# Attention and expert routing on one core: keys of the first batch in four parts, its value products on two column halves, a constant's cast later, row subtractions on VectorE

## Chip, cores, metric

One core of one Trainium2 chip. The metric is the time of one execution on the device in microseconds, the median of the runs of a kernel.

## What is computed

```python
B, N, C = (4, 10048, 128); n_agents = 49
def sm(a, b):                                   # softmax of scaled scores
    s = scale * (a @ b.transpose(0, 2, 1))
...
a2k = sm(agents, k)
agent_v = a2k @ v
q2a = sm(q, agents)
x = q2a @ agent_v                               # 4 x 10048 rows of 128
...
# 4 groups of 4 experts: the best group, in it the best expert, by x @ w_group and x @ w_expert
h = np.maximum(xg[mask_e] @ w1[g, e], 0.0)      # 128 -> 1024
ye = h @ w2[g, e]                               # 1024 -> 128
out[tok_idx] = combined[:, None] * ye
```

The inputs q, k and agents are drawn with a spread of 0.8.

## The kernel before

Each batch is 79 tiles of 128 rows, handled in ten chunks of eight tiles. Products are made of float16 halves: `xh` is the float16 cast of a float32 tile (ScalarE), `xl` the rest (a subtraction, on VectorE or GpSimd, called POOL in the profile), and three matmuls stand for one exact product. Only the sums of exp(scores) times values (`at<-vf,S`) and a few small steps are float32 matmuls; the profile records two instructions for each of these.

A batch has an agent part (scores of the keys, maximum, exponentials `S`, value products), then the choice of the expert that most rows take, that expert's first matrix multiplied by the agents' values (`at<-w1f,at`, giving `wbuf`), and a query part per chunk: scores, `mq` and `ef` (VectorE), exponential (ScalarE), `rows` as high and low half, transposes of `rows` (`at<-ident,rows`), `et`. Then come natural tiles of 512 rows, in eight units each: `first` (line 914) makes two matmuls `ph<-et,wbuf`, `hh` on ScalarE and `hl` on VectorE; `second` (line 930) twelve matmuls `po`. A unit is second up to LAG = 8 units after it was first. The agent and query parts of batch b+1 are woven into the units of batch b. TensorE's, and in the front VectorE's and ScalarE's, instructions keep the order in which the program is written; every engine takes its queue in order.

Only the first batch has nothing to be woven into. Its agent part, the **front** (line 396), is written out in the table ORDER, which sets the order on TensorE, VectorE, ScalarE and of the loads. A letter is a step, the digit a chunk or a part:

- k, v, q: loads of keys, values and the first query chunk. h: the cast to `xh`. l: the subtraction `xl`, on POOL for chunks 1 and 4. s: scores of a key chunk. S: their copy to memory for chunks 3 to 6. M: the chunk's maximum `mch`.
- x, T, a, b, B: a part's maximum: over its chunks (`mx`), transposed by TensorE (`at<-cp,mx`), over its rows (`ma`), spread to all rows by TensorE (`at<-cp,ma`), copied (`mbs`).
- u, e, p, P: subtract the part's maximum, exponential, value products of the first four and of the other tiles. A part has its own sum in PSUM (`acc`), and c adds the parts up with their weights w into `a0`.
- Z, y, r, g, G, t: the first query chunk; g sums its weights over rows on TensorE, between the value products.
- z: that many matmuls of the identity with itself that nobody reads. They write to columns 384 to 511 of the PSUM tile `last`, which also holds the last part's sum.
- A: `main_soon` (line 800): from `a0` the average row, its expert, and that expert's loads `w1f` and `w2f`, issued by SyncE after it has read the choice `which`. D, W, F, R: the agents' values scaled, the expert's matrix, logits and routing of the first chunk. n: steps of the later query chunks.

Parts are of three, three and four chunks. A part's sum is 49 rows high, so a product uses 49 of TensorE's 128 columns; in the agent parts of the other batches (line 365) even tiles go to columns 0 to 48 and odd ones to columns 64 to 112, and the two sums are added at the end.

`query_split` (line 623) makes the high half of `rows` on ScalarE, and for all chunks but the front's first its low half on POOL in pieces of three tiles. POOL also makes all the `xl` of queries. Lines 1238 to 1240, behind the front, load a constant `uf` into a buffer of the tag that `ef` uses (two buffers) and cast it to `upper`, which only the last batch reads (line 987).

In the profile all operations of TensorE, VectorE and ScalarE carry the line of a helper, 138.

## Time and profile before

| | before |
|---|---|
| median of 3 runs | 982.96 us (982.53 to 990.22) |
| profiled execution | 982.84 us, of which the span of the trace is 981.0 us |
| TensorE busy | 923.2 us, 94% of the span |
| VectorE busy | 710.6 us, 72% |
| ScalarE busy | 592.1 us, 60% |
| POOL busy | 420.5 us, 43% |
| granted TensorE clock | 0.99 of full over the span |

A row of the waits says which engine and tile stood, behind "<-" what released it. In the timeline a row is one instruction or a run of equal ones: its start, its duration, and in brackets the idle time of the engine before it and what ended that. Rows of a timeline overlap a little, since an instruction starts before the one ahead of it has drained.

### The profile page before, as it was taken

The numbers are of one execution on the slowest core, as the hardware profiler recorded it, in microseconds if no ns is written. First come the engines' busy times: TensorE is split into PE (matmuls) and PEld (weight loads), VectorE is DVE, ScalarE is ACT, GpSimd is POOL, SyncE is SP. The second block draws the span as 40 slices with busy tenths as digits, with TensorE's granted clock in tenths as the row PEclk, the third lists the DMA queues.
The fourth block names the chain that finished last, engine by engine and source line by source line (L and its number), as shares of the span: only waits on it lengthen the run. The fifth ranks groups of instructions, "written<-read, shape, count | busy, mean of one in ns | idle before, by whom it ended". The sixth has DMA issues, their size and how long they took to land.

```text
span 981.0 us, 30672 instructions
## 1 busy us (share of the span) xinstructions
PE 923.2 (94%) x12943; PEld 721.8 (74%) x12943; DVE 710.6 (72%) x1389; ACT 592.1 (60%) x1073; POOL 420.5 (43%) x681
## 2 busy tenths in 40 slices
PE   7979999999999999999999999999999988989996
PEld 6847887788778788887887788777766656657675
DVE  6677889866987866689785666999976546545563
ACT  5365686777567667856764687564445445434452
POOL 3252465363036244303620452000073786886854
PEclk9988999999999999999999999999999999999998
DMA  9573344630185552018653311134135333433321
GB/s 326 199 250 118 87 149 148 208 122 24 39 297 191 154 161 77 24 37 298 219 153 107 89 41 32 54 143 152 33 120 200 114 117 91 127 99 110 104 79 39
DMA packets 63443, 125.88 MB, mean 128 GB/s; under 512 B 6727, under 2 KB 40904, under 8 KB 60352
## 3 DMA queue, kind: packets, MB, share of 16 engines
q1 hardware_dynamic: 58944, 117.92, 36.0%
q0 software_dynamic: 4352, 5.91, 2.5%
q8 instruction: 103, 1.69, 0.7%
q14 instruction: 44, 0.36, 0.1%
HBM read 90.35 MB, written 33.75 MB: 126 GB/s over the span
## 4 chain that ended last, share of the span: by engine, by line
PE 67%; DVE 12%; issue 3%; ACT 2%; DMA 1%; POOL 1%; another core or an unknown queue 1%; SPq 0%; DVEq 0%; ACTq 0%
PE po L138 34%; PE ph L138 22%; PE at L138 11%; DVE hl L138 5%; DVE oo L138 1%; DMA xf<-kT 1%; DMA w2f<-w 1%; DVE oa L138 1%; POOL xl L257 0%; DVE oh L138 0%; ACT hh L138 0%; DVE mch L138 0%; DVE rd L138 0%; DVE pt L138 0%
## 5 line engine op out<-in xcount | busy, mean ns | idle before, releaser
L138 DVE SCALAR_TENSOR_TENSOR hl<-ph,hh 128x512 f16<-128x512 f32 (+1 forms) x656 | 436.8, 680 | 199.0 <-ACT hh L138 155.6
L138 PEld LDWEIGHTS <-hh 128*128 128x128 f16 x5200 | 423.9, 97 | 167.2 <-issue 22.6
L138 ACT ACTIVATE hh<-ph 128x512 f16<-128x512 f32 (+1 forms) x656 | 378.9, 593 | 247.9 <-PE ph L138 223.0
L138 PE MATMUL po<-wbuf,hh 128*128 128x128 f16 x4816 | 477.1, 219 | 12.5 <-issue 11.6
L138 PE MATMUL po<-wbuf,hl 128*128 128x128 f16 x2408 | 437.4, 219 | 4.1 <-issue 4.0
L138 PE MATMUL ph<-et,wbuf 98*128 98x512 f16 (+1 forms) x1040 | 308.8, 380 | 5.6 <-DVE hl L138 3.3
L257 POOL TENSOR_TENSOR xl<-xf,xh 128x256 f16<-128x256 f32 x280 | 181.3, 679 | 301.0 <-ACT xh L138 294.4
L138 PEld LDWEIGHTS <-hl 128*128 128x128 f16 x2600 | 253.2, 97 | 12.6 <-issue 11.4
L1129 POOL DMA_INDIRECT er<-erow,gidx x68 | 69.6, 1024 | 123.1 <-DVE over L138 110.0
L138 PEld LDWEIGHTS <-wbuf 98*128 98x128 f16 x1216 | 93.2, 99 | 22.8 <-issue 18.8
L138 ACT ACTIVATE xh<-xf 128x1024 f16<-128x1024 f32 x78 | 81.5, 1045 | 42.5 <-PE at L138 32.3
L1166 POOL DMA_INDIRECT out<-oo,sidx x68 | 67.7, 996 | 55.4 <-DVE oo L138 45.2
L633 POOL TENSOR_TENSOR rows<-ef,rows 128x147 f16<-128x147 f32 (+2 forms) x117 | 47.0, 430 | 52.2 <-ACT rows L138 47.1
L138 PEld LDWEIGHTS <-xh 128*128 128x128 f16 x1264 | 55.8, 96 | 5.4 <-issue 3.6
L138 PE MATMUL ph<-ets,wbuf 98*128 98x512 f16 x176 | 53.3, 379 | 0.9 <-issue 0.8
L138 PE MATMUL at<-vf,S 128*49 128x129 f32 (+1 forms) x632 | 52.5, 277 | 1.1 <-ACT S L138 1.1
L1145 POOL MEMSET gap<- 128x320 f16 x136 | 52.3, 385 | 0.3
L138 PEld LDWEIGHTS <-xl 128*128 128x128 f16 x632 | 50.0, 96 | 2.5 <-DVE xl L138 1.3
L138 PE MATMUL at<-agh,xh 128*128 128x49 f16 x545 | 50.8, 184 | 0.8 <-DVE wbuf L138 0.8
L138 DVE TENSOR_TENSOR oo<-po,cw 128x512 f32<-128x512 f32 x65 | 43.9, 675 | 10.4 <-remote 7.2
L138 PE MATMUL at<-agh,xl 128*128 128x49 f16 x545 | 50.6, 184 | 0.3 <-POOL xl L257 0.3
L138 PE MATMUL at<-agl,xh 128*128 128x49 f16 x545 | 50.5, 184 | 0.0
(272 smaller groups left out, 818.5 us busy)
## 6 DMA issues: line engine op xcount, KB each, us to landing
xf<-qT SPq DMA_DIRECT2D x38, 512.0 KB
vf<-v SPq DMA_DIRECT2D x36, 516.0 KB
xf<-kT SPq DMA_DIRECT2D x35, 512.0 KB
out<-oo SPq DMA_DIRECT2D x62, 256.0 KB
wbuf<-wall SPq DMA_DIRECT2D x11, 1024.0 KB
wsg<-wall SPq DMA_DIRECT2D x6, 1024.0 KB
erow<-rows SPq DMA_DIRECT2D x3, 1975.0 KB
w2f<-w SPq DMA_DIRECT2D x7, 512.0 KB
```

Of the source, the lines that this page charges most:

```text
L138: y = f(*a, **k)
L257: eng.tensor_sub(out=xl[:, y], in0=xf[:, y], in1=xh[:, y])
L633: (vec if early else pool).tensor_sub(out=rows[:, w, NA:2 * NA], in0=ef[:, y], in1=rows[:, w, 0:NA])
L1129: ins = pool.indirect_dma_start(out=er[:, q], out_offset=None, in_=erow[b][:, :], in_offset=bass.IndirectOffsetOnAxis(ap=place(b, j * w + ...
L1145: tc.keep_in_program_order(pool.memset(gap, 0.0))
L1166: ins = pool.indirect_dma_start(out=out, out_offset=bass.IndirectOffsetOnAxis(ap=place(x["b"], x["j"] * n + q)[1], axis=0), in_=o[:, q], i ...
```

## The change

- The keys' parts are of one, two, three and four chunks, so that the first part's maximum is known after one chunk; ORDER is written anew for it (its last part is that of before). T makes a second copy of the transposed maxima on partitions 64 to 112, so that maxima, weights and sums stand on both column halves.
- Value products of the front go in turn to columns 0 to 48 and 64 to 112; `a0` is then 113 rows high, and `main_soon` adds its halves by one more float32 matmul with `two` (an identity above an identity) before it goes on. Three halves of PSUM tiles are zeroed at the start.
- A step i is new: 30 matmuls of the identity, written to another PSUM tile, ahead of `at<-w1f,at` (W).
- The load of `uf` and the cast to `upper` go to the end of batch 1's routing.
- The low halves of `rows` of query chunks 1 to 3 of the first batch are made by VectorE in one instruction each.

```diff
+SIDES = HALF + NA
-PARTS = [3, 3, 4]
+PARTS = [1, 2, 3, 4]
+FIRST = 3
-ORDER = ("z44 k0 h0 k1 l0 h1 k2 s0 z8 l1 h2 k3 M0 l2 h3 k4 s2 z6 l3 h4 v0 s1 M2 s3 z10 l4 M1 k5 S3 x0 M3 T0 z8 a0 h5 "
+ORDER = ("z44 k0 h0 k1 l0 h1 k2 s0 z8 l1 h2 k3 v0 M0 T0 z6 a0 l2 b0 z6 B0 h3 k4 s2 z6 u0 e0 l3 h4 s1 p0 M2 s3 l4 P0 M1 k5 S3 x1 "
...
-         "t0 D2 n10 D1 n5 W2 D2 F0 n2 R0").split()
+         "t0 D2 n10 D1 n5 i30 W2 D2 F0 n2 R0").split()
 def front(b, early, order, later):
-        ma, wt, mm, a0, se = [early.tile([NA, w], F32, name=name) for name, w in (("ma", n), ("wt", n), ("mm", 1), ("a0", C + 1), ("se", 1))]
+        ma, wt, mm, a0 = [early.tile([SIDES, w], F32, name=name) for name, w in (("ma", n), ("wt", n), ("mm", 1), ("a0", C + 1))]
-        acc = [(both, both, last)[i][0:NA, y:y + C + 1] for i, y in enumerate((0, C + 1, 0))]
+        acc = [(both, both, both, last)[i][0:SIDES, y:y + C + 1] for i, y in enumerate((0, C + 1, 2 * C + 2, 0))]
+        for x in both, last, small:
+            vec.memset(x[HALF // 2:HALF], 0.0)
...
             elif o == "T":
-                pe.transpose(small[0:NA, 0:P], hold["x"], identf)
+                x = hold["x"] if PARTS[c] > 1 else mch[:, ends[c] - 1]
+                pe.transpose(small[0:NA, 0:P], x, identf)
+                pe.matmul(small[HALF:SIDES, 0:P], x, identf, start=True, stop=True)
...
-                    pe.matmul(acc[i], S[0:m, t], vfs[c % 6][0:m, t - t0], start=todo[i] == whole[i], stop=todo[i] == 1)
+                    side = t % 2 * HALF
+                    pe.matmul(acc[i][side:side + NA], S[0:m, t], vfs[c % 6][0:m, t - t0], start=todo[i] > whole[i] - 2, stop=todo[i] < 3)
...
+            elif o == "i":
+                busy(c, psT[:, 384:512])
 def query_split(b, ci, x, early):
-        for i in range(0, t1 - t0, t1 - t0 if early else 3):
+        whole = early or b == 0 and ci <= FIRST
+        for i in range(0, t1 - t0, t1 - t0 if whole else 3):
...
-            (vec if early else pool).tensor_sub(out=rows[:, w, NA:2 * NA], in0=ef[:, y], in1=rows[:, w, 0:NA])
+            (vec if whole else pool).tensor_sub(out=rows[:, w, NA:2 * NA], in0=ef[:, y], in1=rows[:, w, 0:NA])
 def main_soon(b, early, a0, se, busy):
-        vec.tensor_scalar(out=za, in0=a0[:, C:C + 1], scalar1=1e-9, scalar2=None, op0=ALU.add)
+        ps, psT = bank(b), bank(1)
+        whole = psT[0:NA, P:P + C + 1]
+        pe.matmul(whole, two[0:SIDES], a0, start=True, stop=True)
+        busy(BUSY[0])
+        vec.tensor_scalar(out=za, in0=whole[:, C:C + 1], scalar1=1e-9, scalar2=None, op0=ALU.add)
         vec.reciprocal(out=za, in_=za)
-        vec.tensor_mul(out=se, in0=se, in1=za)
-        ps, psT = bank(b), bank(1)
-        pe.matmul(ps[:, 0:1], a0[:, 0:C], se, start=True, stop=True)
+        av = sm.tile([NA, C], F32, name="av")
+        vec.tensor_scalar(out=av, in0=whole[:, 0:C], scalar1=za, scalar2=None, op0=ALU.mult)
+        pe.matmul(ps[:, 0:1], av, se, start=True, stop=True)
         busy(BUSY[0])
-        av = sm.tile([NA, C], F32, name="av")
-        vec.tensor_scalar(out=av, in0=a0[:, 0:C], scalar1=za, scalar2=None, op0=ALU.mult)
 def rest(b):
         yield from routing(b, 0, NTP)
+        if b == 1:
+            uf = wk.tile([P, P], F32, name="uf", tag="ef")
+            sync.dma_start(out=uf, in_=cpk[:, CUSED:CUSED + P])
         yield from main_of(b, NTP)
+        if b == 1:
+            vec.tensor_copy(out=upper, in_=uf)
...
-    uf = wk.tile([P, P], F32, name="uf", tag="ef")
-    sync.dma_start(out=uf, in_=cpk[:, CUSED:CUSED + P])
-    vec.tensor_copy(out=upper, in_=uf)
```

VectorE near the start of the front, from the first chunk's subtraction `xl` to the subtractions of the part's maximum (`S<-ph,mbs`), before:

```order
L138 TENSOR_TENSOR xl<-xf,xh 128x1024
L138 TENSOR_REDUCE mch<-ph 128x49
L138 TENSOR_TENSOR xl<-xf,xh 128x1024 x2
L138 TENSOR_REDUCE mch<-ph 128x49 x2
L138 TENSOR_REDUCE mx<-mch 128x49
L138 TENSOR_REDUCE mch<-po 128x49
L138 TENSOR_REDUCE ma<-at 49x1
L138 COPY mbs<-at 128x49
L138 TENSOR_TENSOR S<-ph,mbs 128x392
```

The same place after the change:

```order
L140 TENSOR_TENSOR xl<-xf,xh 128x1024
L140 TENSOR_REDUCE mch<-ph 128x49
L140 TENSOR_REDUCE ma<-at 113x1
L140 TENSOR_TENSOR xl<-xf,xh 128x1024
L140 COPY mbs<-at 128x49
L140 TENSOR_TENSOR S<-ph,mbs 128x392
L140 TENSOR_TENSOR xl<-xf,xh 128x1024
L140 TENSOR_REDUCE mch<-ph 128x49 x2
L140 TENSOR_REDUCE mx<-mch 128x49
L140 TENSOR_REDUCE mch<-po 128x49
L140 TENSOR_REDUCE ma<-at 113x1
L140 COPY mbs<-at 128x49
```

One more `ma`, one more `mbs` and the first chunk's `S` stand between the subtractions `xl`; `ma` waits there for TensorE's two transposes.

VectorE at the end of the front, from the query chunks' maxima `mq` to the first unit's `hl`, before:

```order
L138 TENSOR_REDUCE mq<-at 128x8 x2
L138 TENSOR_TENSOR ef<-at,mq 128x392
L138 TENSOR_TENSOR wbuf_104<-at,wbuf_104 128x512 x2
L138 TENSOR_TENSOR rh<-at,rh 98x20
L138 TENSOR_SCALAR main_959<-cp,at 128x16
L138 SCALAR_TENSOR_TENSOR hl<-ph,hh 128x512
```

And after the change:

```order
L140 TENSOR_REDUCE mq<-at 128x8 x2
L140 TENSOR_TENSOR ef<-at,mq 128x392 x2
L140 TENSOR_TENSOR rows<-ef,rows 128x8x49 x2
L140 TENSOR_TENSOR wbuf_104<-at,wbuf_104 128x512 x2
L140 TENSOR_TENSOR rh<-at,rh 98x20
L140 TENSOR_SCALAR main_1001<-cp,at 128x16
L140 SCALAR_TENSOR_TENSOR hl<-ph,hh 128x512
```

Chunk 2's `ef` and the low halves of `rows` of chunks 1 and 2 now stand ahead of the expert's matrix.

POOL from the cast of the first query chunk's `rows` on, before (four `xl` are a chunk, three `rows` are a chunk):

```order
L627 CAST rows<-ef 128x8x49
L257 TENSOR_TENSOR xl<-xf,xh 128x256 x12
L633 TENSOR_TENSOR rows<-ef,rows 128x3x49 x2
L633 TENSOR_TENSOR rows<-ef,rows 128x2x49
L633 TENSOR_TENSOR rows<-ef,rows 128x3x49 x2
L633 TENSOR_TENSOR rows<-ef,rows 128x2x49
L257 TENSOR_TENSOR xl<-xf,xh 128x256 x12
```

And after the change:

```order
L637 CAST rows<-ef 128x8x49
L259 TENSOR_TENSOR xl<-xf,xh 128x256 x24
L644 TENSOR_TENSOR rows<-ef,rows 128x3x49 x2
L644 TENSOR_TENSOR rows<-ef,rows 128x2x49
L259 TENSOR_TENSOR xl<-xf,xh 128x256 x4
```

The six chunks' `xl` follow each other, and the first `rows` that POOL makes are those of chunk 4.

## Rows read from the trace of the kernel before

**Rows 1.** Busy time of each engine (instructions) by stretch, granted clock, DMA share, GB/s.

```profile
20.00:30.00 10.00, 10.00 (x152) 8.70 (x151) 9.09 (x17) 6.29 (x10) 0.00 (x0) 1.00 1.02 402
30.00:44.00 14.00, 13.77 (x150) 12.45 (x147) 6.72 (x18) 4.71 (x10) 5.61 (x9) 1.00 0.51 180
44.00:54.91 10.91, 7.62 (x85) 5.12 (x85) 5.23 (x24) 4.48 (x8) 3.69 (x7) 0.84 0.51 163
54.91:60.05 5.14, 4.96 (x77) 3.24 (x76) 4.29 (x21) 4.08 (x9) 0.00 (x0) 1.00 0.97 361
60.05:72.04 11.99, 9.03 (x112) 6.34 (x112) 9.74 (x26) 9.76 (x19) 7.34 (x12) 0.86 0.61 205
72.04:82.00 9.96, 6.97 (x48) 4.84 (x48) 4.76 (x12) 4.50 (x10) 4.85 (x10) 0.66 0.47 152
82.00:100.00 18.00, 18.00 (x261) 14.40 (x259) 15.71 (x40) 11.61 (x23) 3.83 (x7) 1.00 0.27 83
```

**Rows 2.** Waits of TensorE, 46 to 82 us: us in total, times, longest.

```profile
PE at L138 <- POOL rows L633: 3.0, 1, 3.0
PE at L138 <- DVE rd L138: 2.9, 1, 2.9
```

**Rows 3.** Timeline of VectorE in the front.

```profile
15.63 0.27 DVE L138 TENSOR_REDUCE ma<-at 49x1 f32<-49x128 f32 x1
16.42 0.21 DVE L138 COPY mbs<-at 128x49 f32<-128x49 f32 x1 [0.51 <-PE at L138]
...
25.62 0.57 DVE L138 TENSOR_REDUCE mch<-ph 128x49 f32<-128x392 f32 x1 [0.50 <-PE ph L138]
...
32.56 0.21 DVE L138 COPY mbs<-at 128x49 f32<-128x49 f32 x1 [0.86 <-PE at L138]
...
43.81 0.34 DVE L138 SCALAR_TENSOR_TENSOR a<-at,wt,a 49x129 f32<-49x129 f32 x1 [4.12 <-PE at L138]
...
45.25 0.16 DVE L138 COPY xs<-po 128x1 f32<-128x1 f32 x1 [0.34 <-PE po L138]
...
61.33 1.23 DVE L138 SCALAR_TENSOR_TENSOR wbuf<-w2f,wbuf 128x1024 f16<-128x1024 f32 x1
```

**Rows 4.** Value products, groups by form: the front, 0 to 45 us.

```profile
L138 PE MATMUL at<-vf,S 128*49 128x129 f32 x156 | 19.5, 275 | 0.8 <-ACT S L138 0.8
```

**Rows 5.** The same group in the next batch, on two column halves, 165 to 225 us.

```profile
L138 PE MATMUL at<-vf,S 128*49 128x129 f32 x156 | 10.5, 277 | 0.3 <-ACT S L138 0.3
```

**Rows 6.** Timeline of ScalarE: exponential of the first query chunk.

```profile
36.38 0.53 ACT L138 ACTIVATE ef<-ef 128x392 f32<-128x392 f32 x1 [0.84 <-DVE ef L138]
```

**Rows 7.** Timeline of TensorE: step z, the step after `a0`, transposes of chunk 2's rows.

```profile
42.93 0.84 PE L138 MATMUL at<-ident 128*128 128x128 f16 x12
44.86 0.35 PE L138 MATMUL po<-se,a 49*128 49x1 f32 x2 [1.09 <-DVE se L138]
...
62.96 0.68 PE L138 MATMUL at<-ident,rows 128*98 128x128 f16 x4 [2.91 <-DVE rd L138]
```

**Rows 8.** The sums of step g: group by form, 0 to 45 us.

```profile
L138 PE MATMUL at<-ones,ef 128*49 128x1 f32 x16 | 0.9, 183 | 0.0
```

**Rows 9.** The expert's matrix by form: 46 to 56 us, then 265 to 285 us.

```profile
L138 PE MATMUL at<-w1f,at 128*128 128x512 f32 x4 | 3.6, 1062 | 1.8 <-DMA w1f<-w 1.8
...
L138 PE MATMUL at<-w1f,at 128*128 128x512 f32 x4 | 2.2, 632 | 0.3 <-DVE hl L138 0.3
```

**Rows 10.** Timeline of POOL: rows of chunk 2, then `xl`, then rows of chunk 3.

```profile
61.43 2.21 POOL L633 TENSOR_TENSOR rows<-ef,rows 128x147 f16<-128x147 f32 x3 [8.30 <-ACT rows L138]
...
69.42 5.15 POOL L257 TENSOR_TENSOR xl<-xf,xh 128x256 f16<-128x256 f32 x8 [3.27 <-issue]
74.53 1.18 POOL L633 TENSOR_TENSOR rows<-ef,rows 128x147 f16<-128x147 f32 x3
```

**Rows 11.** Busy time as in group 1, from the first logits to the fourteenth unit's `hl`.

```profile
54.91:80.90 25.99, 19.86 (x223) 13.60 (x223) 18.48 (x56) 17.86 (x34) 11.25 (x19) 0.81 0.65 223
```

**Rows 12.** Timeline of ScalarE: rows of chunk 3, high half.

```profile
71.59 0.53 ACT L138 ACTIVATE rows<-ef 128x392 f16<-128x392 f32 x1
```

More of the change, by code (lines that the diff above doesn't have):

```diff
@@ L383, in agents_of @@
         ps = bank(b)
-        both = slice(0, HALF + NA)
-        pe.matmul(ps[:, 0:NA], av[both, C:C + 1].broadcast_to([HALF + NA, P]), two[both], start=True, stop=True)
+        both = slice(0, SIDES)
+        pe.matmul(ps[:, 0:NA], av[both, C:C + 1].broadcast_to([SIDES, P]), two[both], start=True, stop=True)
         pe.matmul(ps[:, NA:2 * NA], av[both, 0:C], two[both], start=True, stop=True)
@@ L401, in front @@
         n = len(PARTS)
-        ma, wt, mm, a0, se = [early.tile([NA, w], F32, name=name) for name, w in (("ma", n), ("wt", n), ("mm", 1), ("a0", C + 1), ("se", 1))]
+        ma, wt, mm, a0 = [early.tile([SIDES, w], F32, name=name) for name, w in (("ma", n), ("wt", n), ("mm", 1), ("a0", C + 1))]
+        se = early.tile([NA, 1], F32, name="se")
         mbs = early.tile([P, n, NA], F32, name="mbs")
@@ L419, in columns, with busy @@
             return ps[:, 0:n * NA].rearrange("p (t a) -> p t a", a=NA)
-        def busy(n):
+        def busy(n, to=None):
             for _ in range(n):
-                pe.matmul(last[:, 384:512], ident, ident, start=True, stop=True)
+                pe.matmul(last[:, 384:512] if to is None else to, ident, ident, start=True, stop=True)
         pin = tc.keep_in_program_order
@@ L469, in front @@
             elif o == "T":
-                pe.transpose(small[0:NA, 0:P], hold["x"], identf)
+                x = hold["x"] if PARTS[c] > 1 else mch[:, ends[c] - 1]
+                pe.transpose(small[0:NA, 0:P], x, identf)
+                pe.matmul(small[HALF:SIDES, 0:P], x, identf, start=True, stop=True)
             elif o == "a":
-                vec.tensor_reduce(out=ma[:, c:c + 1], in_=small[0:NA, 0:P], axis=AX.X, op=ALU.max)
+                vec.tensor_reduce(out=ma[:, c:c + 1], in_=small[0:SIDES, 0:P], axis=AX.X, op=ALU.max)
             elif o == "b":
-                pe.matmul(small[:, P:P + NA], ma[:, c:c + 1].broadcast_to([NA, P]), identf[0:NA, 0:NA], start=True, stop=True)
+                pe.matmul(small[:, P:P + NA], ma[0:NA, c:c + 1].broadcast_to([NA, P]), identf[0:NA, 0:NA], start=True, stop=True)
             elif o == "B":
@@ L520, in front @@
             elif o == "D":
-                scaled = scaled or agents_scaled(b, psT)
+                scaled = scaled or agents_scaled(b, psT[:, 0:NA])
                 for _ in range(c):
@@ L629, in query_split @@
             act.activation(rows[:, t0:t1, 0:NA], ef, AF.Copy)
-        for i in range(0, t1 - t0, t1 - t0 if early else 3):
-            y = slice(i, t1 - t0 if early else min(i + 3, t1 - t0))
+        whole = early or b == 0 and ci <= FIRST
+        for i in range(0, t1 - t0, t1 - t0 if whole else 3):
+            y = slice(i, t1 - t0 if whole else min(i + 3, t1 - t0))
             w = slice(t0 + y.start, t0 + y.stop)
-            (vec if early else pool).tensor_sub(out=rows[:, w, NA:2 * NA], in0=ef[:, y], in1=rows[:, w, 0:NA])
+            (vec if whole else pool).tensor_sub(out=rows[:, w, NA:2 * NA], in0=ef[:, y], in1=rows[:, w, 0:NA])
         yield
@@ L829, in main_soon @@
         load_weights(b)
-        return psT[:, 0:NA]
+        return psT
     def main_row(b):
```

6 rows, old and new, of the table ORDER are left out of this document.

## The prediction

> **What bounds the kernel now.** I read the busy time by stretch first. From 82 us on TensorE is busy 18.00 of 18.00 us at the full clock [rows 1], and what follows is the same work before and after the change, so whatever is won ahead of 82 us should reach the end whole. Ahead of it there are three different stretches. Up to 43 us TensorE is full (10.00 of 10 us) with VectorE close behind (9.09) [rows 1]. From 44 to 55 us a chain of short steps runs, in which no engine is half busy except TensorE. From 55 to 82 us no engine is full: TensorE is busy 4.96 + 9.03 + 6.97 = 21.0 of 27.1 us, at a mean clock of 1.00, 0.86 and 0.66 [rows 1]. Busy time times clock gives 5.0 + 7.8 + 4.6 = 17.3 us of work at full clock, so this stretch loses 9.8 us: 6.1 by standing, 3.6 by the half clock, 1.2 GHz, that TensorE has there part of the time.
>
> The waits tell where it stands: 2.9 and 3.0 us [rows 2]. The first is put down to VectorE's `rd`, but what starts at 62.96 are the transposes of chunk 2's `rows` [rows 7], whose low half POOL makes from 61.43 on [rows 10]. POOL had stood idle 8.3 us until ScalarE's high half came. For chunk 3 the high half ended at 71.59 + 0.53 = 72.12 [rows 12], but POOL was in two chunks' `xl` until 74.57 and began the low half at 74.53 [rows 10]: POOL's queue was the cause. After both waits the clock is down: 0.86 and 0.66 [rows 1].
>
> **The change part by part.**
>
> *Value products.* On one column half 156 records, 78 products, take 19.5 us, 0.250 each [rows 4]; on two halves, as the next batch does it, 10.5 us, 0.135 each [rows 5]. So 79 products get 9.1 us cheaper on TensorE, but VectorE takes over as the bound. It waits for TensorE 0.50 and 0.86 us behind long runs of products [rows 3]; these 1.4 us go. It gets one more `ma` and `mbs`, 0.27 + 0.21 = 0.5 us, and near the start it waits for the new part's transposes, at most the 0.5 us that it waits in such a round [rows 3]. Net -0.4 us: between -1.4 (the new steps hidden) and +0.8 (loads or ScalarE's new place for the exponential, ahead of a key chunk's cast, cost besides). So the first query chunk's exponential, which ends at 36.38 + 0.53 = 36.91 [rows 6], ends at 36.5. Its sums on TensorE (0.9) [rows 8], then the 15 products that ORDER puts behind them (15 x 0.135 = 2.0) and step z (0.84) [rows 7] follow: 40.2 us. There the last c starts, which waits for step z because both are in `last`; before it started at 43.81 [rows 3]. **-3.6 us** (-4.6 to -2.4).
>
> One rule speaks against this. The Trainium skill (TensorEngine Tiling, Key Properties) says that changing the tiling mode drains TensorE, and the front changes between full-array scores and halves at every burst of four to eight products. The trace of the next batch, where bursts also stand between full-array matmuls, has no such price left in its 0.135 us [rows 5]; so I go by the row, and keep the case that it fails as a rival.
>
> *main_soon.* The halves are added by a matmul between the last c and `za`. The nearest row is the round from `ma` (ends 15.90) over a small float32 matmul to `mbs` (16.42): 0.52 us [rows 3]. With 129 columns in place of 49, and `av` in place of a one-column product ahead of the next matmul, I take **+0.6 us** (0.4 to 0.9) on the 1.44 us from 43.81 to `xs` at 45.25 [rows 3].
>
> *Step i.* Before `w1f` lands TensorE stands 1.8 us, and the two float32 halves behind that take 3.6 us; with no such wait ahead they take 2.2 [rows 9]. Thirty identity matmuls at 0.84 / 12 = 0.07 [rows 7] are 2.1 us, 0.3 more than the wait. They hide in it but for that 0.3: 3.6 - 2.2 - 0.3, **-1.1 us** (+0.3 if the clock falls all the same, -1.4 if the load lands later). VectorE's and ScalarE's work for chunk 2, which now stands ahead of the expert's matrix, fits into the same wait.
>
> *Rows on VectorE, the constant later.* Chunks 1 and 2 have both halves of `rows` before the expert's matrix, and POOL's queue has no `rows` until chunk 4, so both waits of [rows 2] lose their cause. What is late next? From 54.91 us to the end of the fourteenth unit's `hl`, 26.0 us, VectorE works 18.5, ScalarE 17.9 us [rows 11], and TensorE, by the sum above, about 16 at full clock. VectorE loses chunk 2's `ef` and the cast from this stretch and gets chunk 3's `rows`: even. So it becomes VectorE's stretch: not below 18.5 us. One wait I expect to stay: the first `po` need the low half of the second matrix (1.23 us at 61.33 [rows 3]), which stands behind routing steps on VectorE, so that TensorE stands there for 1 to 2 us; most of that overlaps with VectorE being the bound. I take 19.2 us: **-6.8 us** (-7.5 to -2.4, the latter from the first rival). VectorE's remaining routing work finds room behind 82 us, where it has 18.0 - 15.7 = 2.3 us to spare [rows 1].
>
> *At nothing:* the three zeroings and wider weights (VectorE waits for the first load and for TensorE there), and the cast to `upper` in batch 1: its reader is a whole batch later, and if VectorE should wait for that load, some 2 us, up to eight units already made keep TensorE fed.
>
> Sum: -3.6 + 0.6 - 1.1 - 6.8 = -10.9. The profiled execution took 982.84 us with a span of 981.0, 0.12 below the median of 982.96: 982.84 - 10.9 + 0.12 = 972.1 us. One per cent of the median, about what a measurement of this kernel can tell from no change, is 9.8 us: the line is at 973.1.
>
> **The rivals.**
>
> *The clock falls again.* The wait for the second matrix's low half, and one more behind VectorE at chunk 3's transposes, are as long as the 1.8 us that was followed by half clock before (3.6 against 2.2 us [rows 9]). For it: VectorE's queue is full there. Against it: waits of 0.5 to 1.1 us in the front left the clock at 1.00 [rows 1, 3, 7]. Then two waits of 1.8 us replace 2.9 + 3.0, and the half clock's 3.6 us stay: 2.3 us won in place of 6.8. Sum -6.4: 976.6 us.
>
> *The front hardly moves.* VectorE and the key loads set it (DMA share 1.02 in the stretch [rows 1]), the first query chunk is not earlier but later by 0.8, and the loads of values come late for the last bursts: -1.2 in place of -3.6. Sum -8.5: 974.6 us.
>
> *Halves without gain.* By the rule on draining, the short bursts cost as much as before, 0.250 each. TensorE then stays the front's bound until 43.0, with one round of transposes more, some 1 us: +1.0 in place of -3.6. Sum -6.3: 976.7 us. Against it stands [rows 5].
>
> *Slower than before.* With VectorE the bound, TensorE runs dry again and again between 50 and 82 us and has half clock throughout. Its 17.3 us of work become 34.6 in place of 27.1, +7.5. Sum -3.6 + 0.6 - 1.1 + 7.5 = +3.4: 986.4 us. This decides once waits of some 1.8 us come back every few microseconds; half clock for more than 11 of the 17.3 us of work already eats all the gain. Against it: before, with two waits of 3 us, the mean clock was still 0.86 and 0.66 [rows 1].
>
> **How the numbers follow.** The forecast 0.57, its own range 968.5 to 974.5; the clock 0.20; the front 0.12; halves without gain 0.05; slower 0.03; and 0.03 for more than the sum, its best ends together (-4.6 + 0.4 - 1.4 - 7.5 = -13.1, 969.9 us, and below that only if VectorE's work there shrinks too). The range 967.8 to 978.0 leaves out the slower case and little else. Faster by over 1% (below 973.1): 0.8 of the forecast, a quarter of the front's case, and the 0.03 beyond, 0.46 + 0.03 + 0.03, with a little from the rest: 0.54. Slower by over 1%: 0.03. Within: 0.43.
>
> **What would show it.** Right: value products of the front at 0.135 each; the last c at about 40 us; `w1f`'s halves at 2.2 us with no wait of TensorE ahead; no wait of TensorE for `rows` of chunks 2 and 3; VectorE busy over 0.9 of the stretch between the first logits and the fourteenth `hl`, which lasts 18.5 to 20 us. Wrong: a granted clock well below 1.00 behind 50 us, a wait for `wbuf` or `hl` of 1.8 us and more, or new waits behind 82 us that take the gain back.

## The result and the profile after

| | before | changed |
|---|---|---|
| median | 982.79 us of 4 runs (982.53 to 990.22) | 975.35 us of 4 runs (975.20 to 976.45) |
| span of the profiled execution | 981.0 us | 973.4 us |
| ratio to before, 95% interval | | 0.9894 (0.9855 to 0.9933) |

The forecast was 972.1 us, a ratio of 0.989, within 967.8 to 978.0. The kernel is faster by about one per cent; the span shows 7.6 of the 10.9 us that the steps add up to. The question is where the other 3.3 us went.

First the front. Products of the changed kernel by form, 8 to 42 us, then VectorE's timeline and TensorE's:

```profile
L140 PE MATMUL at<-vf,S 128*49 128x129 f32 x156 | 11.3, 279 | 1.7 <-ACT S L140 1.7
```

```profile
39.59 0.35 DVE L140 SCALAR_TENSOR_TENSOR a<-at,wt,a 113x129 f32<-113x129 f32 x1 [2.45 <-PE at L140]
...
41.70 0.16 DVE L140 COPY xs<-po 128x1 f32<-128x1 f32 x1 [0.53 <-PE po L140]
```

```profile
47.98 2.01 PE L140 MATMUL at<-w1f,at 128*128 128x512 f32 x4
...
50.76 0.17 PE L140 MATMUL at<-rh,et 98*128 98x21 f16 x1 [0.63 <-ACT rh L140]
```

A product takes 11.3 / 78 = 0.145 us in place of 0.250 [rows 4]. The last c starts at 39.59 (before 43.81 [rows 3]), the expert's matrix takes 2.0 us in place of 3.6 [rows 9], and the first logits come at 50.76 in place of 54.91 us: 4.15 earlier. Terms one to three of the prediction's sum said 4.1.

Behind them the two kernels have to be compared over the same work. The marks are each tile's `oo`, VectorE's last step for 512 finished rows: the first is at 84.61 us before and 71.53 after, the tenth at 186.44 and 176.70. From the first logits to the tenth both kernels run 1853 matmuls. Busy time and clock from the first logits to the first `oo`, from there to the tenth, and over both, columns as in [rows 1]; before, then changed:

```profile
54.91:84.61 29.70, 23.57 (x285) 16.55 (x285) 21.24 (x66) 20.24 (x38) 12.84 (x22) 0.83 0.57 196
84.61:186.44 101.83, 98.51 (x1572) 79.82 (x1570) 91.23 (x206) 72.95 (x140) 45.66 (x78) 1.00 0.44 133
54.91:186.44 131.53, 122.08 (x1853) 96.37 (x1853) 112.47 (x271) 93.19 (x177) 58.51 (x99) 0.96 0.47 148
```

```profile
50.76:71.53 20.77, 18.80 (x282) 14.17 (x282) 19.87 (x59) 17.92 (x35) 8.85 (x15) 1.00 0.82 285
71.53:176.70 105.17, 99.01 (x1578) 79.90 (x1575) 94.35 (x214) 73.52 (x140) 46.32 (x78) 1.00 0.43 131
50.76:176.70 125.94, 117.82 (x1853) 94.07 (x1853) 114.22 (x272) 91.44 (x175) 55.17 (x93) 1.00 0.50 157
```

Length less TensorE's busy time is how long it stood. To the first `oo`: 6.1 us before, 2.0 after, and the clock rises from 0.83 to 1.00; with nearly the same matmuls, 285 and 282, the stretch is 8.9 us shorter. Behind it the opposite, at the full clock in both: 105.17 in place of 101.83 us, 2.8 us more standing (6.2 in place of 3.3) and 0.5 us more busy time. VectorE has 3.1 us more work there (94.35 in place of 91.23). Over both, 131.53 becomes 125.94: 5.6 us, of which only 1.3 are standing. The other 4.3 are busy time, the same matmuls at a clock of 1.00 in place of 0.96. The waits of TensorE in the whole stretch, before (the two of [rows 2] stand above these) and after:

```profile
PE ph L138 <- DVE mch L138: 1.4, 2, 1.1
PE ph L138 <- DVE hl L138: 1.2, 1, 1.2
PE at L138 <- ACT rh L138: 0.6, 1, 0.6
PE at L138 <- ACT S L138: 0.3, 1, 0.3
PE at L138 <- POOL xl L257: 0.3, 1, 0.3
```

```profile
PE ph L140 <- DVE hl L140: 2.1, 3, 1.2
PE at L140 <- POOL xl L259: 1.4, 4, 0.5
PE po L140 <- DVE wbuf L140: 1.1, 1, 1.1
PE at L140 <- DVE ma L140: 0.9, 1, 0.9
PE ph L140 <- DVE mch L140: 0.9, 2, 0.5
PE at L140 <- ACT S L140: 0.8, 1, 0.8
PE at L140 <- ACT rh L140: 0.6, 1, 0.6
PE at L140 <- DVE hl L140: 0.4, 1, 0.4
PE at L140 <- DVE rows L140: 0.4, 1, 0.4
```

The waits of 2.9 and 3.0 us are gone; in their place come 0.8 us for `rows` and `hl` (the rows with `at`), 1.1 for the second matrix, 2.0 more for `hl` (with `ph`) and `xl`, and 1.4 more for `ma` and `S`. So the first `oo` is 13.1 us ahead of before, the tenth 9.7. Two more places take from that. From 440 to 465 us, where the third batch starts, it goes from 9.85 to 9.06. And between 735 and 750 us, at the switch to the last batch's kept tiles, it goes from 9.0 at the `oo` of 700 us to 7.2 at that of 747 us, two marks up to which the matmuls of the two kernels differ by the same number. The switch (the first matmul on a kept tile, `ph<-ets,wbuf`) is at 744.3 us before and at 735.0 after. The stretch around it, before, then after, same columns:

```profile
740.00:745.00 5.00, 3.63 (x46) 2.67 (x45) 2.63 (x4) 1.29 (x3) 4.06 (x6) 1.00 0.95 388
745.00:750.00 5.00, 4.20 (x41) 2.50 (x40) 1.43 (x3) 2.06 (x5) 1.54 (x2) 1.00 0.78 241
```

```profile
735.00:740.00 5.00, 4.80 (x23) 2.55 (x23) 0.37 (x2) 0.78 (x2) 2.56 (x3) 0.56 0.70 215
740.00:745.00 5.00, 5.00 (x51) 3.84 (x49) 3.77 (x7) 3.46 (x7) 0.00 (x0) 0.76 0.24 95
```

After the change TensorE has 0.56 and 0.76 of its clock here, which loses 4.80 x 0.44 + 5.00 x 0.24 = 3.3 us of work; before it stood 2.2 us but kept the clock.

### The profile page after: what moved, and what is told of

The parts are those of the page before. It is cut to its first block, busy times and chain, and to the rows that moved or that the text cites. A ratio compares the mean times of both kernels' runs of the same rounds, so it can differ in the third digit from the quotient of the medians.

```text
span 973.4 us, 30760 instructions
## 1 busy us (share of the span) xinstructions
PE 917.1 (94%) x12991; PEld 716.0 (74%) x12991; DVE 716.2 (74%) x1397; ACT 592.1 (61%) x1073; POOL 414.6 (43%) x672
## 4 chain that ended last, share of the span: by engine, by line
PE 63%; DVE 15%; issue 4%; POOL 2%; DMA 2%; ACT 1%; another core or an unknown queue 1%; SPq 0%; POOLq 0%; DVEq 0%
PE po L140 32%; PE ph L140 21%; PE at L140 10%; DVE hl L140 6%; DMA xf<-kT 1%; POOL er L1147 1%; DVE oo L140 1%; DVE oh L140 1%; DVE oa L140 1%; ACT hh L140 1%; DVE rx L140 0%; DVE cnt L140 0%; DVE mch L140 0%; POOL xl L259 0%
## 5 line engine op out<-in xcount | busy, mean ns | idle before, releaser
L140 PE MATMUL po<-wbuf,hh 128*128 128x128 f16 x4816 | 477.0, 219 | 12.7 <-issue 10.9
L140 PE MATMUL ph<-et,wbuf 98*128 98x512 f16 (+1 forms) x1040 | 305.7, 376 | 5.6 <-DVE hl L140 4.2
L644 POOL TENSOR_TENSOR rows<-ef,rows 128x147 f16<-128x147 f32 (+1 forms) x108 | 42.5, 422 | 40.8 <-ACT rows L140 40.1
L140 PE MATMUL at<-vf,S 128*49 128x129 f32 (+1 forms) x632 | 44.3, 278 | 2.6 <-ACT S L140 2.5
```

Source lines behind the costliest of these rows:

```text
L140: y = f(*a, **k)
L644: (vec if whole else pool).tensor_sub(out=rows[:, w, NA:2 * NA], in0=ef[:, y], in1=rows[:, w, 0:NA])
```

## The experiments

Theory A: the 3.3 us are swallowed on the way, by VectorE being the bound from 50 to 165 us. Theory B: all that is won ahead of 82 us arrives, and what is missing at the end has other causes. The chips that the runs fell on differ: the kernel before took 953.1 (first four runs and the twelfth: 953.0), 962.6 and 986.7 us there, so ends are compared by the ratio to before on the same chip, the rest by marks in the traces. One table for all profiles (us; "path" is first logits to ninth `oo`, "stood" its length less TensorE's busy time):

| kernel | last c | first logits | ninth oo | path | stood | clock on it | ratio (95%) |
|---|---|---|---|---|---|---|---|
| before | 43.81 | 54.91 | 174.63 | 119.72 | 9.2 | 0.96 | 1 |
| changed | 39.59 | 50.76 | 164.89 | 114.13 | 6.4 | 1.00 | 0.989 (0.986-0.993) |
| e1_low_on_pool | 40.80 | 51.33 | 167.09 | 115.76 | 6.5 | 0.97 | 0.996 (0.994-0.998) |
| e2_no_filler | 39.66 | 50.54 | 164.12 | 113.58 | 6.1 | 1.00 | 0.989 (0.984-0.994) |
| e3_one_half | 47.38 | 59.38 | 173.81 | 114.43 | 5.6 | 0.99 | 1.001 (0.999-1.003) |
| e4_hold_clock | 40.46 | 50.86 | 164.90 | 114.04 | 6.4 | 1.00 | 0.990 (0.987-0.994) |
| e5_constant_front | 39.83 | 51.89 | 166.99 | 115.10 | 5.9 | 0.99 | 0.993 (0.990-0.995) |
| e6_one_max | 40.20 | 51.03 | 164.76 | 113.73 | 5.9 | 0.98 | 0.991 (0.987-0.994) |
| e7_changed_again | 39.89 | 50.58 | 165.36 | 114.78 | 6.0 | 0.99 | 0.991 (0.988-0.994) |
| e8_clock_no_step_i | 39.51 | 49.67 | 163.76 | 114.09 | 6.4 | 1.00 | 0.989 (0.986-0.993) |
| e9_best | 41.15 | 51.41 | 165.11 | 113.70 | 5.8 | 0.98 | 0.987 (0.983-0.990) |
| e10_rows_and_constant_back | 40.61 | 51.34 | 172.49 | 121.15 | 10.2 | 0.94 | 0.995 (0.992-0.998) |
| e11_halves_three_parts | 41.21 | 53.10 | 167.20 | 114.10 | 6.4 | 1.00 | 0.986 (0.982-0.991) |
| e12_clock_at_switch | 39.79 | 49.95 | 162.91 | 112.96 | 6.2 | 1.00 | 0.991 (0.989-0.993) |

How much of this is scatter: VectorE's first `xl`, which waits for the first load, starts between 7.3 and 8.4 us, and all marks of the front move with it. The same changed kernel, profiled twice, has its `oo` of 700 us at 699.58 and 701.39. A difference under 1 us between two single profiles is no finding.

The ninth `oo` is not quite the same work in all: 1681 matmuls lie between it and the first logits in before, e1 and e10, 1687 in e6, e9 and e12, 1701 in the others. At the sixteenth it is 3114 in every profile, and there the paths differ by nearly the same amounts (210.86 before, 205.26 and 205.91 in the two profiles of the changed kernel, 206.88 in e1, 206.23 in e5, 212.29 in e10), except that e6 comes out at 205.22. So the lengths can be compared; how long TensorE stood is compared at the tenth, where before and changed have 1853 each.

**One half (e3).**

```diff
+            vec.memset(x[HALF:P], 0.0)
...
-                    side = t % 2 * HALF
-                    pe.matmul(acc[i][side:side + NA], S[0:m, t], vfs[c % 6][0:m, t - t0], start=todo[i] > whole[i] - 2, stop=todo[i] < 3)
+                    side = 0
+                    pe.matmul(acc[i][side:side + NA], S[0:m, t], vfs[c % 6][0:m, t - t0], start=todo[i] == whole[i], stop=todo[i] == 1)
```

> The changed kernel with all value products on the first column half (the second half's sums are zero); parts, order and the halves' addition stay. If the halves are the front's gain: products at 0.25 us each in place of 0.135, the last c at 43 to 44.5 us in place of 39.6, first logits at 54 to 55. At the end, by theory A (part of it swallowed behind 70 us) +2.5 to +3.5: 978 to 979 us; by rival B +4 and more: 979.5 to 980.5. If the order of the front is what won (four parts), the last c stays below 41 and the end at 976.

```profile
L140 PE MATMUL at<-vf,S 128*49 128x129 f32 x156 | 20.5, 285 | 1.7 <-ACT S L140 1.7
```

0.26 us a product again, and the last c at 47.38, 7.8 us later than in the changed kernel and 3.6 later than before; 43 to 44.5 was expected. The path behind the first logits stays as long as in the changed kernel (114.4), so the 8.6 us by which they come late arrive whole at the ninth `oo` (8.9), more than theory A allowed; the ratio of 1.001 shows the whole of the change gone at the end. What moves everything arrives.

**Halves with the front's order of before (e11).**

```diff
-PARTS = [1, 2, 3, 4]
+PARTS = [3, 3, 4]
```

> The changed kernel with the front's order of before: three parts of keys and the order table of before, with step i; the halves, the rows and the constant as changed. The counterpart, halves away and four parts kept, moved the last c from 39.6 to 47.4 us, 3.6 us behind the kernel before. If the halves alone make the front: last c at 39 to 40.5 us, first logits at 50 to 51.5, the end within 1 us of the changed kernel. If the four parts are needed for it, because with three the waits behind long runs of products stay: last c at 41 to 42.5, first logits 52 to 53.5, the end 1.5 to 2.5 us behind the changed kernel.

The order table of before came with it. Counted from VectorE's first `xl` (7.93 here, 7.37 in the changed kernel, 7.32 before) the last c is 33.28 us behind, against 32.22 and 36.49: the halves win 3.2 us under the old order, the four parts 1.1 more. The first logits come 1.8 us later than in the changed kernel by the same count, but the end does not show it: 0.986 against 0.989 and 0.991 for the changed kernel, intervals overlapping. By these marks (41.21 and 53.10 us) it was the second case of the expectation, by the end the first. The halves make most of the front's gain; what the fourth part adds is too small to be seen at the end.

**Step i and the clock ahead of it (e2, e4, e8).** Fillers are identity matmuls whose result nobody reads. e2 and e4, each against the changed kernel; e8 has the two rows of e4 in `main_soon` and no step i:

```diff
-         ... n5 i30 W2 ...
+         ... n5 W2 ...
```

```diff
+        busy(8, psT[:, 384:512])
         pe.matmul(whole, two[0:SIDES], a0, start=True, stop=True)
-        busy(BUSY[0])
+        busy(11)
...
-         ... n5 i30 W2 ...
+         ... n5 i14 W2 ...
```

> The changed kernel without the thirty identity matmuls of step i. The prediction's step was worth 1.1 us, the trace showed the first logits only 0.6 us earlier than the front alone explains. If the matmuls hold the clock: TensorE waits about 1.8 us for the expert's first matrix, its two float32 halves take 3.6 in place of 2.0 us, the first logits come 0.8 to 1.4 us later (51.6 to 52.2), the end at 975.4 to 976.5 us. If they do nothing: the first logits at 50.2 to 50.9 and the end at 975 us.

> The changed kernel with 8 identity matmuls ahead of the matmul that adds the halves and 11 in place of 3 behind it, and 14 in place of 30 in step i. In the changed kernel TensorE ran at half clock from about 42 to 46 us, behind two new waits of 0.45 and 0.63 us. If these waits are the cause: the 48 score matmuls at 44.4 take 1.4 in place of 2.06 us, the expert's first matrix starts at 46.6 to 47.0 in place of 47.98, the first logits come 1.0 to 1.5 us earlier (49.2 to 49.8). At the end theory A gives -0.5 to -1.0 (974.4 to 974.9 us), rival B -1.0 to -1.5 (973.9 to 974.4). If the clock falls all the same, the scores stay at 2 us and the end at 975 us.

> The changed kernel with 8 identity matmuls ahead of the matmul that adds the halves and 11 in place of 3 behind it, and none in step i. The first four runs, counted from VectorE's first xl (the first load's landing moves by up to 1 us from run to run): holding the clock brought the first logits 0.9 us forward, leaving step i out 0.4 us. If both are real: first logits 42.3 to 42.6 us behind the first xl (43.4 in the changed kernel), the ninth oo 1.0 to 1.5 us earlier than in the changed kernel by the same count. If they are one and the same gain, -0.9; if only the jitter of loads, 0.

Timeline of TensorE in e2, then in e8:

```profile
47.78 1.96 PE L140 MATMUL at<-w1f,at 128*128 128x512 f32 x4 [1.25 <-DMA w1f<-w]
50.54 0.17 PE L140 MATMUL at<-rh,et 98*128 98x21 f16 x1 [0.68 <-ACT rh L140]
```

```profile
46.91 1.96 PE L140 MATMUL at<-w1f,at 128*128 128x512 f32 x4 [1.77 <-DVE ef L140]
49.67 0.17 PE L140 MATMUL at<-rh,et 98*128 98x21 f16 x1 [0.68 <-ACT rh L140]
```

Without the thirty matmuls TensorE waits 1.25 us and then takes 1.96 us for the expert's matrix, not 3.6. So step i does nothing here: the load is issued at 44.1 us in both kernels, and the matrix's first matmul starts at 47.78 without it and at 47.98 with it. The clock ahead of it is another question. From 42 to 46.5 us, the changed kernel, then e4, then e7, which is the changed kernel once more:

```profile
42.00:46.50 4.50, 4.50 (x77) 4.33 (x78) 2.59 (x14) 1.83 (x3) 0.00 (x0) 0.62 0.20 60
```

```profile
42.00:46.50 4.50, 4.28 (x88) 3.92 (x88) 2.81 (x17) 1.95 (x3) 0.88 (x2) 1.00 0.10 31
```

```profile
42.00:46.50 4.50, 4.47 (x96) 4.09 (x96) 3.33 (x17) 2.14 (x3) 0.78 (x2) 1.00 0.17 55
```

With the fillers (e4, e8, e9, e12) the clock stayed full here in four profiles of four. But e7 has the waits of 0.45 and 0.63 us as the first profile had them, no fillers, and the full clock too, and so have e1, e6, e10 and e11. Without fillers it fell in four profiles of nine: the first of the changed kernel, e2, e3 and e5. So it is not shown that the waits bring the clock down, nor that the fillers hold it. What a fall costs is shown: the 48 score matmuls take 2.06 us in the first profile and 1.37 in e4 and e7.

In e4 the gain hides behind a first load that landed a microsecond late. From the last c to the first logits it took 10.4 us, 10.2 in e8, against 11.2 and, without the fall, 10.7 in the two profiles of the changed kernel. e8 beat the changed kernel on the same chip, 951.88 against 954.71 us, with ratios of 0.989 and 0.991 whose intervals overlap.

**Rows and constant (e1, e5, e10).** e1 sets `FIRST = 0`; e5 puts the three lines of `uf` back where they stood; e10 does both:

```diff
-FIRST = 3
+FIRST = 0
...
+    uf = wk.tile([P, P], F32, name="uf", tag="ef")
+    sync.dma_start(out=uf, in_=cpk[:, CUSED:CUSED + P])
+    vec.tensor_copy(out=upper, in_=uf)
     mo = ctx.enter_context(tc.tile_pool(name="mo", bufs=2))
```

> The changed kernel with FIRST at 0: the low halves of the rows of query chunks two to four are POOL's again, in pieces of three tiles, as in the kernel before; everything else as changed. Theory A (what is won ahead of 82 us is partly swallowed between 70 and 165 us, where VectorE is then the bound): the waits for rows come back, the stretch from the first logits to the end of the fourteenth unit's hl goes from 18.2 to 23 to 26 us, but of these 5 to 7 us only about three quarters, less what the switch to the last batch happens to cost, show at the end: 978 to 981 us. Rival B (all that is won ahead of 82 us arrives, and the 5 us missing at the end have other causes): 981 to 983 us. If both waits do not come back (chunk two now has more time), the stretch is at 20 and the end at 976 to 977.

> The changed kernel with the load of the constant and its cast back behind the front, ahead of the units, as in the kernel before. Theory A, as the first four runs leave it: what moves all the work (the front) arrives whole; what only fills TensorE's waits between 55 and 82 us arrives up to what VectorE's own queue allows until some 165 us. Then the cast (0.2 us on VectorE) with its wait for a load, up to 2 us at the head of VectorE's queue, shows at the ninth oo as +0.3 to +2 us against the changed kernel (167.0 to 165.2 in place of 164.9), and the loss of 0.8 to 2.3 us that the four runs showed against before at about 455 us (start of the third batch) is gone if the constant's new place makes it. Rival C (the constant costs nothing anywhere): ninth oo at 164.9, the loss at 455 us stays at 0.8. The end within 1 us of the changed kernel on the same chip in either case.

> The changed kernel with both the low halves back on POOL and the constant's load and cast back ahead of the units. One at a time they cost 1.6 and 1.0 us on the way from the first logits to the ninth oo (115.8 and 115.1 in place of 114.1 us; 119.7 before). If the two together are the prediction's third term, they cost 4 to 6 us (118 to 120). If they only add up, 116.5 to 117, and the other 2.7 us of the gain in this stretch come from what the changed order does ahead of it (the second chunk's exponential and both row halves ahead of the expert's matrix, and a clock that is still high). The ratio to before 0.994 to 0.998 in the first case, 0.992 to 0.995 in the second.

The path is 115.8 us with the rows back, 115.1 with the constant back, and 121.2 with both, 1.4 longer than before. Against the changed kernel's first profile one alone costs 1.0 to 1.6 us and the two together 7.0, against its second (e7) 0.3 to 1.0 and 6.4: one alone is hardly more than scatter. At the end the two cost a little less, 0.4 to 0.6 per cent by the ratios, 4 to 6 us; e1 costs more, 5.3 and 7.3 us against e4 and e2 on the same chip, of which the marks at 700 us have only 2.6 and 1.7. What the last batch adds or takes there stays open. Waits of TensorE from the first logits to 90 us in e10, then in e1, then in e5:

```profile
PE at L140 <- POOL rows L644: 6.5, 3, 3.5
```

```profile
PE at L140 <- POOL rows L644: 1.9, 1, 1.9
```

```profile
PE po L140 <- DVE wbuf L140: 1.9, 1, 1.9
...
PE at L140 <- DVE rows L140: 0.2, 1, 0.2
```

The timeline of VectorE says why they go together; e10, then the changed kernel:

```profile
46.96 0.55 DVE L140 TENSOR_TENSOR ef<-at,mq 128x392 f32<-128x392 f32 x1
54.00 0.56 DVE L140 TENSOR_TENSOR ef<-at,mq 128x392 f32<-128x392 f32 x1
57.19 0.23 DVE L140 CAST upper<-uf 128x128 f16<-128x128 f32 x1 [1.02 <-DMA uf<-cpk]
```

```profile
46.99 1.03 DVE L140 TENSOR_TENSOR ef<-at,mq 128x392 f32<-128x392 f32 x2
```

With the constant behind the front, chunk 2's `ef` stands behind the expert's matrix (54.0 us; 58.5 before) and not with chunk 1's ahead of it. Then its rows are late, and POOL, slow and busy, makes them later still: 6.5 us of waits and a clock of 0.94. With the constant moved, POOL has chunk 2's rows done in time and only chunk 3's are waited for; with the rows on VectorE, chunk 2's late `ef` is made good at once. Either edit closes most of the hole, and theory A's reading of e1 falls: up to the tenth `oo` e1 stands no longer than the changed kernel (6.8 and 8.1 us), it only loses 0.03 of the clock.

Behind the first `oo` the row subtractions on VectorE have a price. From the first `oo` to the tenth, e10, then e5, which differs from it in these subtractions alone:

```profile
82.88:184.30 101.42, 98.14 (x1567) 79.48 (x1565) 91.16 (x207) 73.05 (x140) 45.89 (x77) 1.00 0.43 134
```

```profile
74.49:178.80 104.31, 98.91 (x1577) 79.80 (x1573) 93.63 (x212) 73.65 (x140) 46.76 (x80) 1.00 0.43 131
```

TensorE stands 3.3 us in e10 and 5.4 in e5. In all three kernels with the rows on POOL (before, e1, e10) it is 3.3 to 3.4 us, in the eleven with them on VectorE 5.4 to 6.2. The loss of lead at 455 us is there in e5 too (8.32 to 7.46), so it is not the constant's. Whether chunk 2's `ef` moves because `uf` holds one of the two buffers of its tag, or because the order of the queues comes out another way, was not tried apart.

**Less work for VectorE (e6).**

```diff
-        if ci:
-            vec.tensor_max(out=mch[:, ci], in0=mch[:, ci], in1=mch[:, ci - 1])
...
-        mx = st["mch"][:, len(chunks) - 1]
+        mx = sm.tile([P, NA], F32, name="mx")
+        vec.tensor_reduce(out=mx, in_=st["mch"].rearrange("p c a -> p a c"), axis=AX.X, op=ALU.max)
```

> The changed kernel with the nine running maxima per batch over the key chunks (0.47 us each on VectorE, 4.2 us a batch, all of batch 1's between 100 and 165 us) replaced by one reduction per batch over all chunks (estimate 0.6 to 0.7 us from the front's 0.26 for two columns and 0.56 for eight): 3.5 us less for VectorE. Theory A (VectorE is the bound up to 165 us): the ninth oo comes 2 to 3.5 us earlier than in the changed kernel, at 161.4 to 163 us, TensorE's busy share between 100 and 165 us rises above 0.97, and the end is 2 to 3.5 us earlier. Rival B (TensorE's own work bounds there, its waits come from the loads or POOL): the ninth oo and the end within 0.7 us of the changed kernel.

Waits of TensorE in e6, 70 to 166 us:

```profile
PE at L140 <- DVE ma L140: 1.5, 1, 1.5
PE at L140 <- POOL xl L259: 1.4, 4, 0.5
PE ph L140 <- DVE mch L140: 1.1, 1, 1.1
PE ph L140 <- DVE hl L140: 0.8, 1, 0.8
```

The nine maxima, 4.2 us in the changed kernel, became one reduction of 1.0 us. These 3.2 us less work on VectorE shorten the path by 0.4 and 1.05 us against the two profiles of the changed kernel, and by 0.04 and 0.7 us at the sixteenth `oo`: no more than scatter. At the end e6's median is 2.1 us below the changed kernel's on the same chip, but the runs' ranges overlap (952.1 to 955.3 and 951.2 to 956.7 us), and at the `oo` of 700 us the profiles differ by 0.35 us only. So VectorE's load is not the bound of this stretch, and theory A falls as it was put. TensorE's own work is: 107.7 of 114.1 us at the full clock. The 6.4 us left are a dozen waits, none over 1.2 us, for VectorE, POOL and ScalarE in turn; take one away and the next is there (here 1.5 us for `ma`, which now waits for the one reduction at the end). Theory B does not hold either: the lead shrinks from 13.1 to 9.7 us on the way. What is left of theory A is that the waits behind the first `oo` come with the row subtractions on VectorE (e10 and e5, changed kernel and e1). Why they come there, when less work on VectorE does not take them away, was not tried.

**The changed kernel on another chip (e7).**

> The changed kernel once more, beside the others on one chip, because the first four runs fell on a chip on which the kernel before took 953 us in place of 983. If the chips differ only in the last batch's kept tiles (725 us and later), its oo marks up to 720 us repeat those of the first profile within 0.5 us, and its end stands some 8 to 10 us ahead of the kernel before there. If the change is worth less on that chip, 5 us or less.

Ahead of before by 7.9 us there, 0.991. Its marks up to 475 us are 0.4 to 1.0 us later than in the first profile, those from 640 to 715 us 1.8 us, more than the 0.5 expected; the clock falls at the switch here too (0.67 from 735 to 740 us).

**The best of these together (e9), and fillers at the switch (e12).** e9 is e8 with e6; e12 is e9 with, ahead of the first kept tile:

```diff
+        if j == 0:
+            ps = bank()
+            for _ in range(24):
+                tc.keep_in_program_order(pe.matmul(ps[:, 0:P], ident, ident, start=True, stop=True))
         run(x, None, late[0] if late else None)
```

> The version with 19 identity matmuls around the matmul that adds the halves and none in step i, together with the one reduction per batch in place of the running maxima. On the last chip these were 2.8 and 2.1 us faster than the changed kernel at the end, though at the oo marks of 700 us only 3.0 and 0.35. If the second gain is real: 4 to 5 us ahead of the changed kernel, a ratio to before of 0.986 to 0.988. If only the first is: 0.989. In both cases the first logits at 42.3 to 42.9 us behind VectorE's first xl.

> The version of the ninth run with 24 identity matmuls in TensorE's queue at the switch to the last batch's kept tiles, just ahead of the wait for the reloaded weights (1.1 to 2.1 us long in the profiles, followed by half clock for 3 to 7 us in four of the eleven profiles of changed kernels). If that wait sets the clock and the fillers lie within it: granted clock 1.00 throughout 725 to 750 us, first matmul on ets not later than 9.6 to 9.9 us behind the third write of the kept weights, and a ratio to before of 0.984 to 0.987, 0 to 2 us ahead of the ninth run. If the fillers push the last units before the wait out, so that the wait comes behind them all the same: up to 1.7 us later, 0.987 to 0.989. A single profile at full clock does not by itself show the first, since more than half of the profiles had it without fillers.

e9 has a ratio of 0.987 (0.983 to 0.990), 973.78 us against 986.68 there: nominally ahead of both kernels, clearly so only of the kernel before. e12 missed: 0.991, where 0.984 to 0.989 was expected. The scheduler put the fillers ahead of the last unit, so they ended at 728.2 us and TensorE waited all the same. Timeline of TensorE in e12, and its stretch behind:

```profile
726.69 1.50 PE L140 MATMUL at<-ident 128*128 128x128 f16 x24
...
731.14 0.60 PE L140 MATMUL ph<-ets,wbuf 98*128 98x512 f16 x2 [2.39 <-DMA wbuf<-wall]
```

```profile
730.00:735.00 5.00, 3.86 (x26) 2.67 (x27) 1.38 (x2) 1.49 (x3) 4.06 (x6) 0.69 1.02 388
```

What it waits for is a chain of transfers. SyncE's queue in the changed kernel:

```profile
723.88 0.33 SPq L1139 DMA_DIRECT2D wall<-wsg  x1
...
728.03 0.35 SPq L1167 DMA_DIRECT2D wbuf<-wall  x1
```

Three kept experts' matrices are written to memory and one is read back, 1 MB each; the read is issued behind the third write. From that write to the first matmul on `ets` it takes 9.9 us before, 11.1 in the changed kernel's first profile and 9.6 in e2, e7 and e8. In eleven of the profiles TensorE gets there ahead of the read and stands 1.1 to 3.0 us for it; in the kernel before, e10 and the first profile of the changed kernel it does not. Around the switch the clock fell in five of the thirteen profiles of changed kernels (the changed kernel twice, e5, e11, e12). What decides that was not found; the test with e12 was not one, since the wait stayed.

## Why the prediction came out as it did

**Value products: right.** Predicted 0.135 us each and the last c at 40.2; measured 0.145 and 39.6. As expected VectorE became the bound in the middle of the front, 9.90 of 10 us from 20 to 30 us, while TensorE fell from 10.00 to 7.63. The rival by which the halves win nothing is refuted: e3 shows 0.26 us a product on one half. Its rule, the Trainium skill's (TensorEngine Tiling, Key Properties) that a change of mode drains TensorE, has no price to be seen here: the short bursts between full-array scores run at 0.145 us, against 0.135 in the next batch [rows 5]. Of the two parts of this edit, the halves carry most of it (e11).

**main_soon: right, with a fall of the clock not foreseen.** The last c to `xs` went from 1.44 to 2.11 us, +0.67 against +0.6. But behind its new waits of 0.45 and 0.63 us TensorE had 0.62 of its clock from 42 to 46.5 us, and the 48 score matmuls there took 2.06 us; at the full clock they take 1.37 (e4, e7). The price is these 0.7 us. The prediction had set waits of this length aside, since in the front of before such waits left the clock at 1.00; of the waits that it names, though, only the 1.09 us of [rows 7] is TensorE's, the others are VectorE's. As the same kernel kept its clock in e7 behind the same waits, the fall in the first profile was chance as far as these runs show.

**Step i: the size right by luck, the reason wrong.** The matrix does take 2.0 in place of 3.6 us, but e2 and e8 have that without step i, behind waits of 1.25 and 1.77 us. The step of the prediction that said TensorE must be kept at work across the wait failed. Why the clock held there and not before the change, behind a wait of 1.8 us, is open.

**Rows and constant: right in size, with the wrong half of the reason.** Predicted -6.8; undoing both lengthens the path by 7.0 (e10), 2.4 of it standing and 4.6 busy time for the same 1853 matmuls up to the tenth `oo`, that is, clock. Against the kernel before, 5.6 of it show, because e10 has a path 1.4 us longer than before; its profile has 13.7 us at the half level on the path, that of before 10.2, and these 3.4 us more are by themselves worth 1.7. The forecast's marker, the fourteenth `hl`, was met and passed: 18.17 us in place of 19.2, with VectorE busy 17.27 us of it. But the rows on VectorE were not the main thing. The constant's place was, as much: it keeps chunk 2's exponential ahead of the expert's matrix, and either edit does most of the work alone (e1, e5). The prediction read [rows 10] as POOL waiting for ScalarE's high half and put "even" on VectorE's account; it did not ask why that high half came so late.

**What failed: "whatever is won ahead of 82 us should reach the end whole".** The first `oo` is 13.1 us ahead, more than the 10.9 of the sum, but the tenth only 9.7: between the two TensorE stands 6.2 in place of 3.3 us. The sum had this at nothing, because VectorE's remaining work was to find room behind 82 us, in the 2.3 us that it had to spare there. It has 3.1 us more work there, and the waits come with its row subtractions (5.4 us in e5, 3.3 in e10). Room alone would not have helped: e6 gave VectorE 3.2 us more, TensorE still stood 5.5 us, and the path hardly moved. Two more losses were not in the sum. At 440 to 465 us TensorE waits 1.4 in place of 0.8 us for VectorE's half of the third batch's matrix; with what lies around it, 0.8 us. e8 lost only 0.2 there, so this one comes and goes. And at the switch to the kept tiles, with the half clock behind it, the lead goes from 9.0 to 7.2 us. In e7 the lead over the same profile of before rises there, from 7.2 to 8.7, so this loss belongs to the one profile. Together that leaves the 7.6 us of the span. That the time lies so near the forecast is in part luck: more was won up to the first `oo` than the sum had, and some of it was lost again in places that the sum had at nothing.

**The rivals.** In the first profile the clock did not fall again between the first logits and the ninth `oo` (1.00), but it fell in two places where the prediction had not looked, ahead of the expert's matrix and at the switch. In e7 it did fall there, at 57.4 us for 3.4 us, and the path is 0.65 us longer. The front did move. Slower than before came nowhere near, since TensorE's longest wait on that path is 1.2 us. The sum of the second rival, 974.6 us, should read 974.5, which changes nothing.

## What to carry to other kernels

Compare two kernels over the same work, from a common start to a mark up to which they have run the same number of instructions: a scheduler moves other work across a mark, and counted to the ninth tile, with 20 matmuls more in the changed kernel, the new waits come to 1.4 us where to the tenth, with equal work, they are 2.8. Look for a gain not only where it is made but behind it: 13 us ahead at the first tile were 10 at the tenth. When a stretch is bound by one engine's own work, what is left are many short waits for different engines, and relieving one of them wins little. Before blaming an engine that is late, follow its input back: here the late engine was POOL, and the step that made it late was a constant's load and cast ahead of it. Undo edits in pairs as well as singly, since two that each close the same hole look cheap one by one. Profile the same kernel twice before a fall of the clock is put down to an edit: here it fell at 42.7 us in one profile and not in the other.

## What the runs showed of the hardware

The kernel before took 953 to 987 us on the chips used. The changed kernel, profiled on two of them, has the same marks up to 725 us within some 2 us, but spans of 973.4 and 952.9 us. Its last batch on the first chip, then on the other (e7), columns as in [rows 1]:

```profile
800.00:850.00 50.00, 45.16 (x527) 32.59 (x528) 28.05 (x42) 23.83 (x41) 38.65 (x57) 1.00 0.33 100
```

```profile
800.00:850.00 50.00, 47.15 (x547) 34.08 (x548) 29.10 (x44) 24.32 (x43) 44.56 (x65) 1.00 0.43 116
```

On the first, TensorE stands 31 times in 800 to 900 us, 0.4 us at most, 8.6 us in all, with nothing in the trace that releases it; on the other 14 times, 3.4 us. One of POOL's indirect transfers takes 1.0 us on both. The cause is open.

The length of a wait does not tell whether the clock falls behind it. Waits of 0.45 and 0.63 us in `main_soon` were followed by 0.62 of the clock in one profile of the changed kernel and by 1.00 in the other (e7), waits of 1.25, 1.77 and 1.79 us for the expert's matrix (e2, e8, e11) by full clock, the wait of 1.8 us before the change by the half. At the switch 2.1 us (e8) left it at 1.00 and 1.7 us (e7) brought it to 0.67.
